# Expert tiles of 256, 320 and 128 tokens by rank, in place of 256 and 128 with one spare tile

## The chip, the cores and the metric

One core of one Trainium2 chip runs the whole program as one launch. The metric is the time of an execution on the device in microseconds. Three runs of the kernel before gave 782.85, 783.31 and 784.54 us.

## What is computed

Three layers follow each other: an attention within clusters (2 batches, 8 heads, 768 tokens, head size 64), a mixture of experts in which each token goes to one expert, and a bilinear layer. The middle one is what the change is about:

```python
logits = x @ w_gate                    # x: 1536 x 512, 8 experts
expert_idx = np.argmax(logits, axis=1)
...
    xe = x[mask]                       # the tokens of expert e
    h = np.maximum(xe @ w1[e], 0.0)    # 512 -> 1024
    ye = h @ w2[e]                     # 1024 -> 512
    out[mask] = gate_w[mask, None] * ye
```

How many tokens an expert has is known only when the attention has run. On the reference's own inputs, drawn with its default seed, experts 0 to 7 have 198, 119, 169, 188, 162, 192, 206 and 302 tokens.

## The kernel before

**Precision.** Matrix operands are kept as two parts, a rounded high part and the remainder ("hi" and "lo" for weights, "xh" and "xl" for tokens, "hh" and "hl" for the hidden layer), and each product is three matmuls. For a chunk of weights, which is 512 KB in a tile "raw", ACT casts "hi" (line 139) and DVE subtracts to get "lo" (line 145). An expert has eight chunks, four of w1 and four of w2.

**Routing.** Near the end of the attention the tokens are written to a buffer "xs" in DRAM, one region of 1536 rows for each expert, by indirect DMAs on POOL's queue (`scatter`). The first 256 rows of each region are set to zero earlier by DMAs from SP (line 888). `tables` then works out on DVE, from the counts, which expert stands at which place, where its output begins, and what is left over. Its first step is emitted at once, the others are spread over the expert stage, one for some of the calls of `tick`.

**The expert stage.** It goes through `SEQ` (line 72): nine places, 0, 1, 2, 7, 3, 8, 4, 5, 6. Places 0 to 6 are windows of 256 tokens (`window`, line 1088), with the tokens as the moving side: 96 matmuls of 256 columns for h, 96 for y. Place 7 is a tile of 128 tokens (`tile_of`, line 1140) with the weights as the moving side: 48 matmuls of 256 columns, eight transposes of h (line 1163), 24 matmuls of 512 columns (line 1176). It takes the expert with the fewest tokens. Place 8 is a tile of the same kind for the expert with most tokens beyond its window; it loads that expert's eight chunks once more, and its registers come from the table "wi". What is still left after that goes to a loop of 128-row tiles (line 1321), whose number of turns is read at run time. Expert 0 is always at place 0, since its weights are loaded before the counts are known.

**The order of work.** Each engine runs its instructions in the order in which they are written. `tick` is called 16 times in a window or a tile; each call lets `advance` split up to two more chunks, which puts a "hi" into ACT's queue and a "lo" into DVE's and lets SP issue the next load of "raw" (four buffers). The calls `nxt` in the second half of a window (`window(..., (1, 3))`) put in the transposes of the next place's tokens (`win_xt`, line 1075): four matmuls on PE into "xt", the copy "xh" on ACT, the subtraction "xl" on DVE. `store` (line 1134) copies y to "yt" in SBUF, two halves on ACT and DVE. A tile's output is transposed first ("yt_t", line 1203), in the next place.

**PSUM.** In the expert stage the tag "h" has four banks, "xt" two, and "y" takes two.

Of the kernel before, what the change touches and what calls it, by code (L numbers as in the profile page):

```python
# [23 lines left out]
W = 256  # L24
WS = 128
CH = 1024
# [3 lines left out]
def cluster_attention__then__moe__then__bilinear_kernel(  # L30
# [41 lines left out]
    SEQ = [0, 1, 2, E - 1, 3, E, 4, 5, 6]  # L72
    MOE2 = 8 * (E + 1)
# [85 lines left out]
    fmp = cp.tile([128, 128], F32, name="fmp")  # L159
# [8 lines left out]
    ahead = cp.tile([128, E, E], BF16, name="ahead")  # L168
    auxt = [cp.tile([128, NT, 2], U32, name=f"auxt{b}") for b in range(B)]

    def routing_constants():
        def iota(t, pattern, base=0, mult=0):
            nc.gpsimd.iota(t, pattern=pattern, base=base, channel_multiplier=mult,
                           allow_small_or_imprecise_dtypes=True)

        nc.gpsimd.memset(ones, 1.0)
# [11 lines left out]
        place_in = cp.tile([128, E], F32, name="place_in")  # L188
        n_s = SEQ.index(E - 1)
        nc.gpsimd.tensor_scalar(out=place_in, in0=ecol, scalar1=float(n_s), scalar2=1.0, op0=ALU.is_ge, op1=ALU.mult)  # L190
        nc.gpsimd.tensor_tensor(out=place_in, in0=place_in, in1=ecol, op=ALU.add)
        nc.gpsimd.memset(place_in[:, E - 1:E], float(n_s))
        nc.gpsimd.tensor_tensor(out=ahead, in0=place_in.unsqueeze(1).to_broadcast([128, E, E]),
                                in1=place_in.unsqueeze(2).to_broadcast([128, E, E]), op=ALU.subtract)
# [447 lines left out]
    def tables(later):  # L642
# [8 lines left out]
        m = cp.tile([128, 8], F32, name="wm")  # L651
        e1 = cp.tile([128, E], F32, name="we1")
        od = cp.tile([128, E], F32, name="od")
        nc.vector.tensor_reduce(out=m[:, 0:1], in_=cnt[:, 1:E], axis=AX.X, op=ALU.min)
        nc.vector.scalar_tensor_tensor(out=e1[:, 1:E], in0=cnt[:, 1:E], scalar=m[:, 0:1], in1=efirst[:, 0, 1:E],
                                       op0=ALU.is_le, op1=ALU.mult)
        nc.vector.tensor_reduce(out=m[:, 1:2], in_=e1[:, 1:E], axis=AX.X, op=ALU.max)
        nc.vector.tensor_scalar(out=m[:, 2:3], in0=m[:, 1:2], scalar1=-1.0, scalar2=float(E), op0=ALU.mult, op1=ALU.add)
        nc.vector.scalar_tensor_tensor(out=od, in0=ecol, scalar=m[:, 2:3], in1=ecol, op0=ALU.is_ge, op1=ALU.add)
        nc.vector.tensor_copy(od[:, E - 1:E], m[:, 2:3])  # L660
        ri = cp.tile([128, 3, E], I32, name="ri")
# [6 lines left out]
        hot = tp.tile([128, E, E], F32, name="hot")  # L668
        t8 = tp.tile([128, E, E], F32, name="t8")
        o8 = tp.tile([128, 2, E], F32, name="o8")  # L670
        off = cp.tile([128, E], F32, name="offs")
        nc.vector.tensor_tensor(out=hot, in0=od.unsqueeze(2).to_broadcast([128, E, E]),
                                in1=ecol.unsqueeze(1).to_broadcast([128, E, E]), op=ALU.is_equal)
# [6 lines left out]
        nc.vector.tensor_copy(ri[:, 2, :], o8[:, 1, :])  # L680
        yield
# [4 lines left out]


        cap = tp.tile([128, E], F32, name="cap")
        key = tp.tile([128, E], F32, name="key")
        nc.vector.tensor_scalar(out=cap, in0=hot[:, E - 1, :], scalar1=float(WS - W), scalar2=float(W),  # L690
                                op0=ALU.mult, op1=ALU.add)
        nc.vector.tensor_tensor(out=key, in0=cnt, in1=cap, op=ALU.subtract)
        nc.vector.tensor_scalar(out=key, in0=key, scalar1=0.0, scalar2=2048.0, op0=ALU.max, op1=ALU.mult)
        nc.vector.tensor_tensor(out=key, in0=key, in1=cnt, op=ALU.add)
        yield
        nc.vector.tensor_reduce(out=m[:, 0:1], in_=key, axis=AX.X, op=ALU.max)
        nc.vector.scalar_tensor_tensor(out=e1, in0=key, scalar=m[:, 0:1], in1=efirst[:, 0, :],
                                       op0=ALU.is_ge, op1=ALU.mult)
        nc.vector.tensor_reduce(out=m[:, 1:2], in_=e1, axis=AX.X, op=ALU.max)
        nc.vector.tensor_scalar(out=e1, in0=e1, scalar1=m[:, 1:2], scalar2=None, op0=ALU.is_equal)  # L700
        yield
        rs = cp.tile([128, E], F32, name="wrs")
        nc.vector.scalar_tensor_tensor(out=rs, in0=cnt, scalar=float(-WS), in1=cap, op0=ALU.add, op1=ALU.min)
        w3 = cp.tile([128, 3, E], F32, name="w3")
        nc.vector.tensor_tensor(out=w3[:, 1, :], in0=rs, in1=erow, op=ALU.add)
        nc.vector.tensor_tensor(out=w3[:, 2, :], in0=rs, in1=off, op=ALU.add)
        nc.vector.tensor_copy(w3[:, 0, :], ecol)
        nc.vector.tensor_tensor(out=w3, in0=w3, in1=e1.unsqueeze(1).to_broadcast([128, 3, E]), op=ALU.mult)
        wv = cp.tile([128, 3], F32, name="wv")
        nc.vector.tensor_reduce(out=wv, in_=w3, axis=AX.X, op=ALU.add)  # L710
        wi = cp.tile([128, 3], I32, name="wi")
        nc.vector.tensor_copy(wi, wv)
        regs["wi"] = wi
# [17 lines left out]
        nc.vector.tensor_scalar(out=n[:, 1:2], in0=n[:, 0:1], scalar1=1.0, scalar2=None, op0=ALU.is_gt)  # L731
        nc.vector.tensor_tensor(out=n[:, 0:1], in0=n[:, 0:1], in1=n[:, 1:2], op=ALU.mult)
# [337 lines left out]
    def win_load(w, src, n):  # L1070
        xw[w] = mp.tile([128, 2, DM], F32, tag="xw", name=f"xw{w}", bufs=2)
        for a in range(n // 128):
            nc.sync.dma_start(out=xw[w][:, a, :], in_=src[128 * a:128 * a + 128])

    def win_xt(w, n, a):

        if a == 0:
            xh[w] = mp.tile([128, DB, W], F32R, tag="xh", name=f"xh{w}", bufs=2)
            xl[w] = mp.tile([128, DB, W], F32R, tag="xl", name=f"xl{w}", bufs=2)
        x = mps.tile([128, 512], F32, tag="xt", name=f"xt{w}_{a}", bufs=2)  # L1080
        for d in range(DB):
            nc.tensor.transpose(x[:, 128 * d:128 * d + 128], xw[w][:, a, 128 * d:128 * d + 128], ident)
        xv = x.rearrange("p (d t) -> p d t", d=DB)
        oh, ol = xh[w][:, :, 128 * a:128 * a + 128], xl[w][:, :, 128 * a:128 * a + 128]
        nc.scalar.copy(out=oh, in_=xv)
        nc.vector.tensor_tensor(out=ol, in0=xv, in1=oh.bitcast(F32), op=ALU.subtract)

    def window(w, n, c0, tick, nxt, at):
        hh, hl = [], []
        y = mps.tile([128, DB, W], F32, tag="y", name=f"y{w}")  # L1090
# [15 lines left out]
        for fb in range(FB):  # L1106
# [364 lines left out]
```

## Time and profile before

| | |
|---|---|
| Runs | 782.85, 783.31, 784.54 us (median 783.31) |
| The profiled execution | 783.25 us, its span 781.1 us |
| Attention, routing | 0 to 279.4 us |
| Expert stage, first to last matmul | 279.36 to 475.29 us |
| Bilinear layer | 479.4 us to the end |
| PE busy in the span | 761.6 us (98%) |
| DVE, ACT, POOL busy | 523.2, 355.6, 156.9 us |

The profiled execution's time is 0.06 us below the median of the runs; the 2.15 us between its time and its span lie outside the instructions. Start times in the rows further down are from the span's start. Matmuls overlap in the pipeline, so the cost of one is read from the distance between starts, not from its duration.

### The profile page before, as it was taken

To read this page: it belongs to the slowest core of one execution; us is meant where nothing else is said; L and a number is where in the kernel's file an instruction comes from. 1 tells how busy PE (TensorE), PEld (TensorE's weight loads), DVE (VectorE), ACT (ScalarE), POOL (GpSimd) and SP (SyncE) were. 2 spreads that over 40 slices of the span, in tenths; PEclk is the share of its full clock that TensorE was granted. 3 is DMA by queue.
4 is the path that set the end of the run, shared out by engine and by line. 5 is a ranking of instruction groups with operands and counts; after the bars stand their busy time and mean duration, and the time that the engine had idled before them with its cause. 6 is when DMAs were issued, how large, how long until landed. Compare 5 with 4: busy or idle time off the path is not lost. (4 is left out here: it accounts for less than half of the span.)

```text
span 781.1 us, 12589 instructions
## 1 busy us (share of the span) xinstructions
PE 761.6 (98%) x4731; PEld 629.9 (81%) x4731; DVE 523.2 (67%) x947; ACT 355.6 (46%) x677; POOL 156.9 (20%) x164
## 2 busy tenths in 40 slices
PE   9999999999999999999999998999999999999996
PEld 8676676665766789998999997888888888888885
DVE  5867868778687778877686686766456765625323
ACT  6767666675666447547575432323132121210100
POOL 7623221415110410000007000211212112102011
PEclk9999999999999999999999999999999999999999
DMA  6685955737410168858789854322222220001011
GB/s 144 143 192 180 277 134 117 170 92 198 108 49 1 43 215 272 267 173 270 255 275 158 229 166 111 111 79 81 81 55 82 56 80 0 1 1 55 0 55 54
DMA packets 76302, 98.17 MB, mean 126 GB/s; under 512 B 28368, under 2 KB 49360, under 8 KB 76240
## 3 DMA queue, kind: packets, MB, share of 16 engines
q1 hardware_dynamic: 73792, 91.01, 42.2%
q0 software_dynamic: 2304, 6.31, 2.2%
q8 instruction: 38, 0.62, 0.4%
q14 instruction: 24, 0.20, 0.1%
q10 hardware_dynamic: 144, 0.03, 0.0%
HBM read 70.32 MB, written 10.50 MB: 103 GB/s over the span
## 5 line engine op out<-in xcount | busy, mean ns | idle before, releaser
L1408 PE MATMUL ab<-yh,hi 128*128 128x512 f32 x288 | 113.0, 392 | 0.0
L1408 PE MATMUL ab<-yh,lo 128*128 128x512 f32 x288 | 112.6, 391 | 0.0
L1415 DVE TENSOR_TENSOR ga<-ga,ab 128x512 f32<-128x512 f32 x36 | 24.7, 686 | 127.8 <-PE ab L1408 102.1
L464 DVE TENSOR_REDUCE nm<-s 128x1 f32<-128x768 f32 x96 | 91.5, 953 | 18.1 <-PE s L462 14.0
L145 DVE TENSOR_TENSOR lo<-raw,hi 128x1024 fp32r<-128x1024 f32 x70 | 84.8, 1223 | 22.4 <-ACT hi L139 21.7
L471 ACT ACTIVATE pr<-s,nm 128x768 f32<-128x768 f32 x96 | 87.0, 906 | 18.4 <-DVE nm L464 17.9
L462 PE MATMUL s<-ks,qs 128*128 128x512 f32 (+1 forms) x384 | 91.6, 361 | 0.3 <-ACT pr L471 0.3
L1414 ACT COPY ga<-ab 128x512 f32<-128x512 f32 x36 | 21.1, 586 | 151.9 <-PE ab L1408 151.9
L485 PE MATMUL t<-ident,pr 128*128 128x128 f32 x576 | 82.8, 277 | 3.8 <-DVE pt L491 2.2
L485 PEld LDWEIGHTS t<-ident,pr 128*128 128x128 f32 x576 | 64.6, 141 | 25.1 <-issue 10.8
L139 ACT CAST hi<-raw 128x1024 fp32r<-128x1024 f32 x70 | 72.2, 1048 | 17.4 <-DMA raw<-in_moe_w 17.3
L145 POOL TENSOR_TENSOR lo<-tmp,hi 128x512 fp32r<-128x512 f32 x28 | 38.2, 1365 | 204.6 <-ACT hi L139 204.6
L1408 PE MATMUL ab<-yl,hi 128*128 128x512 f32 x288 | 77.0, 389 | 0.0
L501 PE MATMUL o<-pt,vn 128*64 128x384 f32 (+1 forms) x432 | 74.5, 468 | 0.0
L491 DVE COPY pt<-t 128x384 f32<-128x384 f32 x94 | 51.8, 551 | 27.2 <-PE t L485 27.0
L489 ACT COPY pt<-t 128x384 f32<-128x384 f32 x98 | 46.7, 478 | 46.5 <-PE t L485 46.0
L462 PEld LDWEIGHTS s<-ks,qs 128*128 128x128 f32 x384 | 58.5, 190 | 9.6 <-issue 4.4
L1127 PE MATMUL y<-hh,hi 128*128 128x256 f32 x224 | 63.8, 285 | 0.0
L1408 PEld LDWEIGHTS ab<-yh,hi 128*128 128x128 f32 x288 | 54.5, 189 | 11.4
L1408 PEld LDWEIGHTS ab<-yh,lo 128*128 128x128 f32 x288 | 54.5, 189 | 11.3
L1408 PEld LDWEIGHTS ab<-yl,hi 128*128 128x128 f32 x288 | 54.1, 188 | 11.2
L1127 PE MATMUL y<-hh,lo 128*128 128x256 f32 x224 | 62.9, 281 | 0.0
(328 smaller groups left out, 1543.4 us busy)
## 6 DMA issues: line engine op xcount, KB each, us to landing
raw<-in_moe_w SPq DMA_DIRECT2D x72, 512.0 KB, 4.8
raw<-in_moe_w_a SPq DMA_DIRECT2D x12, 512.0 KB, 3.7
raw<-in_moe_w_b SPq DMA_DIRECT2D x12, 512.0 KB, 3.7
raw<-in_moe_w_out SPq DMA_DIRECT2D x12, 512.0 KB, 3.4
qs<-hiq SPq DMA_DIRECT2D x14, 384.0 KB, 4.8
ks<-hik SPq DMA_DIRECT2D x28, 192.0 KB, 4.8
xs<-zero SPq DMA_DIRECT2D x8, 512.0 KB, 5.5
xw<-xs SPq DMA_DIRECT2D x14, 256.0 KB, 5.0
```

The costliest lines, as they stand in the source:

```text
L139: nc.scalar.copy(out=hi, in_=raw)
L145: eng.tensor_tensor(out=lo, in0=raw, in1=hi.bitcast(F32), op=ALU.subtract)
L462: nc.tensor.matmul(sc[:, c0:c1], lhsT=w, rhs=ks[s, h][:, i, c0:c1], start=(i == 0), stop=(i == 1))
L464: nc.vector.tensor_reduce(out=nm, in_=sc[:, 0:S], axis=AX.X, op=ALU.max, negate=True)
L471: nc.scalar.activation(out=pr, in_=sc[:, 0:S], func=AF.Exp, bias=nm, scale=1.0, accum_out=sums[p][:, t, h:h + 1])
L485: nc.tensor.transpose(x[:, 128 * n:128 * n + 128], pr[:, 128 * kb:128 * kb + 128], ident)
L489: nc.scalar.copy(out=dst, in_=src)
L491: nc.vector.tensor_copy(dst, src)
L501: nc.tensor.matmul(o[64 * h:64 * h + 64, 0:n], lhsT=vn[:, h, kb, :], rhs=pt_t[p, g, h][:, kb, 128 * j0:128 * j0 + n], start=(kb == 0), sto ...
L1127: nc.tensor.matmul(y[:, d, 0:n], lhsT=a_[:, fb % 2, 128 * d:128 * d + 128], rhs=b_[:, 0:n], start=(fb == 0 and d % 2 == 0 and i == 0), sto ...
L1408: nc.tensor.matmul(p_, lhsT=a_[:, d, f0:f0 + 128], rhs=b_[d], start=(i == 0), stop=(i == len(seq) - 1))
L1415: nc.vector.tensor_tensor(out=ga, in0=ga, in1=ab[1], op=ALU.mult)
```

## The change

`SEQ` has eight places instead of nine, in the order of their numbers. The experts are ranked by their number of tokens on DVE (expert 0 first, always; the others by count). Place 1 takes the fullest of the others and is a window of 320 columns; place 3 takes the emptiest and is the tile of 128; the rest are windows of 256. The spare tile, its table "wi" and its loads are gone; what does not fit goes to the loop, now from the first tile on. A window of 320 loads a third piece of 64 rows ("xw1b"), transposes it in a third call of `nxt`, and accumulates y in four banks, two of "y" and two of "h", which `store_wide` copies with eight instructions. SP also sets 64 more rows of each expert's region to zero.

```diff
+WL = 320
...
-    SEQ = [0, 1, 2, E - 1, 3, E, 4, 5, 6]
-    MOE2 = 8 * (E + 1)
+    LARGE, LITTLE = 1, 3
+    RANK = [0, 1, 2, E - 1] + list(range(3, E - 1))
+    SIZE = [WL if n == LARGE else WS if n == LITTLE else W for n in range(E)]
+    SEQ = list(range(E))
+    MOE2 = 8 * E
...
+        nc.vector.scalar_tensor_tensor(out=key, in0=cnt, scalar=8.0, in1=ties, op0=ALU.mult, op1=ALU.add)
+        nc.vector.tensor_tensor(out=more, in0=key.unsqueeze(1).to_broadcast([128, E, E]),
+                                in1=key.unsqueeze(2).to_broadcast([128, E, E]), op=ALU.is_gt)
+        nc.vector.tensor_reduce(out=rank, in_=more, axis=AX.X, op=ALU.add)
+        nc.vector.tensor_tensor(out=hot, in0=by_rank.unsqueeze(2).to_broadcast([128, E, E]),
+                                in1=rank.unsqueeze(1).to_broadcast([128, E, E]), op=ALU.is_equal)
+        nc.vector.tensor_tensor(out=t8, in0=hot, in1=ecol.unsqueeze(1).to_broadcast([128, E, E]), op=ALU.mult)
+        nc.vector.tensor_reduce(out=od, in_=t8, axis=AX.X, op=ALU.add)
...
-        nc.vector.tensor_scalar(out=n[:, 1:2], in0=n[:, 0:1], scalar1=1.0, scalar2=None, op0=ALU.is_gt)
-        nc.vector.tensor_tensor(out=n[:, 0:1], in0=n[:, 0:1], in1=n[:, 1:2], op=ALU.mult)
...
+        at(NU + 2 + 2 * e, lambda e=e: nc.sync.dma_start(
+            out=xs[e * NTOK + W:e * NTOK + WL, :].rearrange("r (h d) -> (r h) d", h=2), in_=zero[:, 0:DM // 2]))
...
     def win_load(w, src, n):
...
+        if n > W:
+            xw[w].append(mp.tile([128, DM], F32, tag="yn", name=f"xw{w}b"))
+        for a in range(-(-n // 128)):
+            m = min(128, n - 128 * a)
+            nc.sync.dma_start(out=xw[w][a][0:m], in_=src[128 * a:128 * a + m])
...
     def window(w, n, c0, tick, nxt, at):
...
+        if n > W:
+
+            ys = [y.rearrange("p d t -> p (d t)")[:, 512 * i:512 * i + n] for i in range(2)]
+            ys += [mps.tile([128, 512], F32, tag="h", name=f"y{w}_{i}", bufs=4)[:, 0:n] for i in range(2)]
...
+    def store_wide(ys, n, at, at2):
+        for d in range(DB):
+            copy = nc.scalar.copy if d < 2 else nc.vector.tensor_copy
+            copy(out=yt[:, d, bass.ds(at, W)], in_=ys[d][:, 0:W])
+            copy(out=yt[:, d, bass.ds(at2, n - W)], in_=ys[d][:, W:n])
...
-        if t < 18 and t % 4 == 2 or 18 <= t < 48 and t % 2 == 0 or t >= 97:
+        if t < 18 and t % 4 == 2 or 18 <= t < 48 and t % 2 == 0 or t >= 16 * (LITTLE + 1) + 2:
...
-            y = window(r, W, 8 * pos, tick, nxt, (1, 3))
-            store(y, W, ov[r])
+            y = window(r, size(r), 8 * pos, tick, nxt, (1, 3, 5))
+            if size(r) > W:
+                store_wide(y, size(r), ov[r], ov[r, 1])
+            else:
+                store(y, W, ov[r])
```

How this moves instructions stands below for two places. The first is ACT's queue in the second half of place 0, where the tokens of place 1 are prepared ("xh1" from the transposes "xt1") between the casts of chunks 12 to 15 and the store of place 0. Before:

```order
L1085 CAST xh1_3708<-xt1_0_3710 128x4x128
L139 CAST hi_12_3719<-raw_12_3611 128x1024
L1256 TENSOR_LOAD ri_3422
L1085 CAST xh1_3708<-xt1_1_3753 128x4x128
L139 CAST hi_13_3760<-raw_13_3653 128x1024
L139 CAST hi_14_3766<-raw_14_3676 128x1024
L139 CAST hi_15_3798<-raw_15_3682 128x1024
L1135 ISA
L1135 COPY yt_3449<-y0_3487 128x2x256
L1116 ACTIVATE hh1_0_3853<-h1_0_3840 128x256
```

And of the change:

```order
L1082 CAST xh1_3722<-xt1_0_3724 128x4x128
L143 CAST hi_12_3734<-raw_12_3625 128x1024
L1264 TENSOR_LOAD ri_3436
L1082 CAST xh1_3722<-xt1_1_3768 128x4x128
L143 CAST hi_13_3775<-raw_13_3667 128x1024
L143 CAST hi_14_3781<-raw_14_3690 128x1024
L1082 CAST xh1_3722<-xt1_2_3811 128x4x64
L143 CAST hi_15_3820<-raw_15_3696 128x1024
L1143 ISA
L1143 COPY yt_3463<-y0_3501 128x2x256
L1114 ACTIVATE hh1_0_3875<-h1_0_3862 128x320
```

A third piece of "xh1" now stands behind the casts of chunks 13 and 14, and the first matmul of place 1 reads all 320 columns of "xh1".

The second place is SP's queue at the start of place 0, where the tokens of place 1 are loaded ("xw1") ahead of chunks 8 and on. Before:

```order
L102 DMA raw_7_3472<-in_moe_w2 128x2x512
L1256 TENSOR_LOAD ri_3422 x3
L1073 ISA
L1073 DMA xw1_3527<-xs_70 128x512
L1073 ISA
L1073 DMA xw1_3527<-xs_70 128x512
L102 ISA
L102 DMA raw_8_3561<-in_moe_w1 128x4x256
```

And of the change:

```order
L106 DMA raw_7_3486<-in_moe_w2 128x2x512
L1264 TENSOR_LOAD ri_3436 x3
L1069 ISA
L1069 DMA xw1_3541<-xs_70 128x512
L1069 ISA
L1069 DMA xw1_3541<-xs_70 128x512
L1069 ISA
L1069 DMA xw1b_3542<-xs_70 64x512
L106 ISA
L106 DMA raw_8_3575<-in_moe_w1 128x4x256
```

The load of the third piece, 64 rows or 128 KB, has moved in ahead of chunk 8.

## Rows read from the trace of the kernel before

**Rows 1.** The page: busy time and share of the span, of PE.
```profile
PE 761.6 (98%) x4731; PEld 629.9 (81%) x4731; DVE 523.2 (67%) x947; ACT 355.6 (46%) x677; POOL 156.9 (20%) x164
```

**Rows 2.** Windows view by place, columns as the first line: place 1, both tiles, all nine.
```profile
core 0: us, PE busy (x) PEld busy (x) DVE busy (x) ACT busy (x) POOL busy (x), PEclk, DMA share, GB/s
...
303.91:328.05 24.14, 24.04 (x203) 23.84 (x201) 22.12 (x55) 15.00 (x22) 0.00 (x0) 1.00 0.85 277
...
351.39:365.50 14.11, 13.25 (x90) 11.85 (x89) 10.61 (x14) 11.33 (x17) 0.00 (x0) 1.00 0.86 290
...
389.27:402.52 13.25, 13.24 (x90) 11.85 (x89) 11.41 (x14) 11.30 (x17) 0.00 (x0) 1.00 0.76 253
...
sum 195.93, PE 193.19 PEld 189.58 DVE 150.36 ACT 109.20 POOL 14.63; mean PE 21.47 PEld 21.06 DVE 16.71 ACT 12.13 POOL 1.63
```

**Rows 3.** Waits of PE from 276 to 482 us: total us, times, longest.
```profile
PE warm L790 <- SPq L1321: 2.3, 1, 2.3
...
PE xt L1082 <- issue: 0.9, 1, 0.9
PE h L1103 <- ACT xh L1240: 0.7, 1, 0.7
```

**Rows 4.** Timeline of PE, expert stage: start, duration, instruction, count.
```profile
303.91 0.29 PE L1103 MATMUL h<-xh,hi 128*128 128x256 f32 x1
...
401.12 0.40 PE L1176 MATMUL y<-hi,sh 128*128 128x512 f32 x1
...
402.52 0.28 PE L1103 MATMUL h<-xh,hi 128*128 128x256 f32 x1
...
414.04 0.28 PE L1127 MATMUL y<-hh,hi 128*128 128x256 f32 x1
...
417.35 0.60 PE L1082 MATMUL xt<-ident,xw 128*128 128x128 f32 x4
417.71 0.36 PE L1127 MATMUL y<-hh,hi 128*128 128x256 f32 x1
```

**Rows 5.** The chain that ended last, in order of time, bilinear layer: start, us, count.
```profile
494.33 5.44 PE ab L1408 x24
```

**Rows 6.** Timeline of ACT, end of place 0; in brackets idle before, and its releaser.
```profile
303.79 1.05 ACT L139 CAST hi<-raw 128x1024 fp32r<-128x1024 f32 x1 [0.94 <-DMA raw<-in_moe_w]
305.10 1.06 ACT L139 CAST hi<-raw 128x1024 fp32r<-128x1024 f32 x1 [0.26 <-DMA raw<-in_moe_w]
306.06 0.57 ACT L1135 COPY yt<-y 128x512 f32 x1
306.53 0.38 ACT L1116 ACTIVATE hh<-h 128x256 fp32r<-128x256 f32 x1
```

**Rows 7.** Timeline of DVE, ends of places 0 and 1.
```profile
304.87 1.22 DVE L145 TENSOR_TENSOR lo<-raw,hi 128x1024 fp32r<-128x1024 f32 x1 [0.76 <-ACT hi L139]
...
328.25 0.69 DVE L1136 COPY yt<-y 128x512 f32 x1 [0.71 <-PE y L1127]
```

**Rows 8.** Timeline of SP's DMA issues, attention and start of place 0.
```profile
61.54 2.25 SPq L888 DMA_DIRECT2D xs<-zero  x3
74.19 2.68 SPq L428 DMA_DIRECT2D qs<-hiq  x2
...
285.00 0.94 SPq L1073 DMA_DIRECT2D xw<-xs  x2
```

**Rows 9.** Timeline of PE, attention.
```profile
188.75 0.55 PE L485 MATMUL t<-ident,pr 128*128 128x128 f32 x3 [0.35 <-ACT pt L489]
190.62 0.55 PE L485 MATMUL t<-ident,pr 128*128 128x128 f32 x3 [1.33 <-DVE pt L491]
```

**Rows 10.** Windows view of the stretch behind those two waits (columns as rows 2).
```profile
191.25:195.17 3.92, 3.92 (x15) 1.58 (x14) 2.71 (x5) 1.93 (x4) 2.92 (x3) 0.56 0.78 282
```

**Rows 11.** DMA issues of the page: queue, count, KB each, median us to landing.
```profile
raw<-in_moe_w SPq DMA_DIRECT2D x72, 512.0 KB, 4.8
...
xw<-xs SPq DMA_DIRECT2D x14, 256.0 KB, 5.0
```

More of the change, by code (lines that the diff above doesn't have):

```diff
@@ L168, in cluster_attention__then__moe__then__bilinear_kernel @@
     ahead = cp.tile([128, E, E], BF16, name="ahead")
+    by_rank = cp.tile([128, E], F32, name="by_rank")
+    ties = cp.tile([128, E], F32, name="ties")
     auxt = [cp.tile([128, NT, 2], U32, name=f"auxt{b}") for b in range(B)]
@@ L174, in iota @@
                            allow_small_or_imprecise_dtypes=True)
+        fmp = ap.tile([128, 128], F32, name="fmp")
         nc.gpsimd.memset(ones, 1.0)
@@ L186, in routing_constants @@
         iota(jcol, [[0, E], [1, NJ]])
[L188 to L194, printed above, removed]
-        nc.gpsimd.tensor_scalar(out=ahead, in0=ahead, scalar1=0.0, scalar2=1.0, op0=ALU.is_lt, op1=ALU.mult)
+        nc.gpsimd.tensor_tensor(out=ahead, in0=ecol.unsqueeze(1).to_broadcast([128, E, E]),
+                                in1=ecol.unsqueeze(2).to_broadcast([128, E, E]), op=ALU.subtract)
+        nc.gpsimd.tensor_scalar(out=ahead, in0=ahead, scalar1=0.0, scalar2=1.0, op0=ALU.is_lt, op1=ALU.mult)
+        iota(by_rank, [[1, E]])
+        nc.gpsimd.memset(by_rank[:, LITTLE:LITTLE + 1], float(E - 1))
+        iota(by_rank[:, LITTLE + 1:E], [[1, E - LITTLE - 1]], LITTLE)
+        iota(ties, [[-1, E]])
+        nc.gpsimd.memset(ties[:, 0:1], float(16 * NTOK))
         for b in range(B):
@@ L649, in tables @@
         nc.vector.tensor_copy(cnt, c[:, 0:E])
[L651 to L661, printed above, removed]
+        key = ap.tile([128, E], F32, name="key")
+        more = ap.tile([128, E, E], F32, name="more")
+        rank = cp.tile([128, E], F32, name="rank")
+        hot = cp.tile([128, E, E], F32, name="hot")
+        t8 = ap.tile([128, E, E], F32, name="t8")
+        od = ap.tile([128, E], F32, name="od")
+        nc.vector.scalar_tensor_tensor(out=key, in0=cnt, scalar=8.0, in1=ties, op0=ALU.mult, op1=ALU.add)
[6 more added lines that the diff above has]
+        nc.vector.tensor_reduce(out=od, in_=t8, axis=AX.X, op=ALU.add)
+        ri = cp.tile([128, 4, E], I32, name="ri")
         nc.vector.tensor_copy(ri[:, 0, :], od)
@@ L667, in tables @@
         tp = later()
[L668 to L669 removed]
+        t8 = tp.tile([128, E, E], F32, name="t8b")
         o8 = tp.tile([128, 2, E], F32, name="o8")
         off = cp.tile([128, E], F32, name="offs")
[L672 to L673 removed]
         nc.vector.tensor_tensor(out=t8, in0=hot, in1=cnt.unsqueeze(1).to_broadcast([128, E, E]), op=ALU.mult)
@@ L680, in tables @@
         nc.vector.tensor_copy(ri[:, 2, :], o8[:, 1, :])
+        nc.vector.tensor_scalar(out=ri[:, 3, :], in0=o8[:, 1, :], scalar1=float(W), scalar2=float(NTOK + W - (WL - W)),
+                                op0=ALU.add, op1=ALU.min)
         yield
@@ L688, in tables @@
         cap = tp.tile([128, E], F32, name="cap")
[L689 to L713, printed above, removed]
+        e1 = cp.tile([128, E], F32, name="we1")
+        nc.vector.tensor_scalar(out=cap, in0=rank, scalar1=float(RANK[LARGE]), scalar2=float(WL - W),
+                                op0=ALU.is_equal, op1=ALU.mult)
+        nc.vector.tensor_scalar(out=e1, in0=rank, scalar1=float(RANK[LITTLE]), scalar2=float(WS - W),
+                                op0=ALU.is_equal, op1=ALU.mult)
+        nc.vector.tensor_tensor(out=cap, in0=cap, in1=e1, op=ALU.add)
+        nc.vector.tensor_scalar(out=cap, in0=cap, scalar1=float(W), scalar2=None, op0=ALU.add)
         yield
@@ L1090, in window @@
         y = mps.tile([128, DB, W], F32, tag="y", name=f"y{w}")
+        ys = [y[:, d, 0:min(n, W)] for d in range(DB)]
         seqs = [[(i, d) for d in range(DB) for i in range(2)] + [(2, d) for d in range(DB)]]
@@ L1142, in tile_of @@
         hp_ = [mps.tile([128, 512], F32, tag="h", name=f"h{w}_{i}", bufs=4) for i in range(2)]
-        hs = mp.tile([128, F], F32, tag="ys", name="hs", bufs=2)
-        hh = [mp.tile([128, W], F32R, tag=f"hh{i}", name=f"sh{i}") for i in range(FB // 2)]
-        hl = [mp.tile([128, W], F32R, tag=f"hl{i}", name=f"sl{i}") for i in range(FB // 2)]
+        hs = mp.tile([128, F], F32, tag="ys", name="hs")
+        hh = [mp.tile([128, WL], F32R, tag=f"hh{i}", name=f"sh{i}") for i in range(FB // 2)]
+        hl = [mp.tile([128, WL], F32R, tag=f"hl{i}", name=f"sl{i}") for i in range(FB // 2)]
         def h_part(c):
@@ L1194, in tile_of @@
             y_part(fb)
-        yn = mp.tile([128, F], F32, tag="ys", name="yn", bufs=2)[:, 0:DM]
+        yn = mp.tile([128, DM], F32, tag="yn", name="yn")
         nc.scalar.copy(out=yn, in_=y)
```

50 lines of the change are left out of this document (25 added, 25 removed).

## The prediction

> **What bounds the kernel now.** The page comes first: PE is busy for 98% of the span, with DVE at 67% and ACT at 46% [rows 1]. So a change is worth what it takes from PE's queue or puts in front of it. The windows view, cut at the first matmul of each place, says the same of the expert stage: of its 195.93 us PE is busy for 193.19 [rows 2]. PE's waits make up the rest. Two of them matter here: 0.9 us in front of the transposes "xt" inside the tile of place 3, which is why that tile takes 14.11 us and the spare one 13.25 [rows 2, 3], and 2.3 us at the loop's entry, which the change leaves alone [rows 3].
>
> The distances between starts give PE's price of a column. Six matmuls of 512 columns go from 401.12 to 402.52, 0.233 us each, and the next 96 of 256 columns from 402.52 to 414.04, 0.120 us each [rows 4]. In the bilinear layer 24 of 512 columns take 5.44 us, 0.227 each [rows 5]. So 256 columns more cost 0.107 to 0.113 us, and 64 columns a quarter of that, 26.7 to 28.3 ns.
>
> **The spare tile goes.** Its stretch lasts 13.25 us [rows 2]. It also holds the two transposes of the next place's tokens, which stay; but its own one and that of its output, which stand in the places before and after, go with it, and four transposes cost the same 0.36 us (417.35 to 417.71) either way [rows 4]. The sum: **-13.25 us**. Its eight chunks, 4.2 MB, their casts and subtractions go too. I cost that at nothing, since PE did not wait for them elsewhere in the stage.
>
> **The wide window.** It has 192 matmuls with 64 columns more: 192 x 26.7 to 28.3 ns is 5.1 to 5.4 us. I take **+5.3**, nearer to the price seen in this stage. The third piece of its tokens needs four transposes of 64 rows, between half and the whole of 0.36 us [rows 4]: **+0.3**.
>
> The first of these terms is where a rule speaks against the rows. In a stream of weight loads and matmuls the distances are 0.120 and about 0.23 us here [rows 4, 5]. The Trainium skill ("TensorE: Matmul & The Clock Gate", Back-to-back issue gap) gives 81 ns at 128 columns and 131 ns at 512 for such a stream. By that, 64 columns cost 8 ns, the wide window an estimated 1.6 us, and the sum below would be 3.7 us better. The trace disagrees by its 0.227 and 0.233, and I go by the trace.
>
> **A new wait at the start of place 1.** Each engine keeps its order, so the place of the third copy "xh1" counts. It stands behind ACT's casts of chunks 13 and 14 (order of ACT above). In the trace the second of these waits 0.94 us for its weights and runs from 303.79 to 304.84, at the very end of place 0; the next matmul of PE starts at 303.91 [rows 4, 6]. The cast of chunk 15 and the store of y followed there, and the store began at 306.06 although y had been ready for two microseconds: this is what standing behind a late chunk costs [rows 6]. None of it held PE, because no next matmul needed it. Now one does. The third copy has 256 elements to a partition, as the activation of 0.38 us [rows 6], and can end at 305.2 at the earliest; place 1 would be ready at 303.91 + 0.3 = 304.2. PE waits 1.0 us. The third subtraction "xl1" stands behind "lo" of chunk 14, which ended at 306.09 [rows 7]; it ends by 306.5, and PE needs it eight matmuls after 305.2, at 306.4: 0.1 more. Third, SP now issues the extra load ahead of chunk 8 (order of SP above); an issue takes 0.47 us [rows 8], and if chunk 14 becomes late by all of that, so does PE. From below: if chunk 14 landed 0.94 us earlier, the wait would be gone. So 0 to 1.6 us, and I take **+1.2**.
>
> **What I cost at nothing.**
> - The banks. Two of the wide window's y products use banks of "h", and the third h of place 2 waits until DVE has copied them. It starts 24 x 0.120 = 2.9 us after place 2 does. DVE's copies have 640 columns in four instructions; before, 512 columns took 0.69 us, and DVE had been idle for 0.71 us when it began [rows 7]. Even twice 0.69 leaves 1.5 us of cover. If DVE came to that point later than this cover, PE would wait in place 2.
> - DVE in place 1. It was busy for 22.12 of 24.14 us [rows 2]. The place now lasts 5.3 us longer with hardly more to do, so the weights, loaded at a share of 0.85 [rows 2], get ahead rather than fall behind.
> - The ranking. DVE has eight small instructions for it where eight were before, some with 64 elements instead of 8. PE's first wait in the stage is for ACT's "xh", 0.7 us [rows 3], which needs none of them.
> - Eight more zeroing DMAs on SP. They cost no more than the larger ones, 2.25 us for three [rows 8], some 6 us in all. After the last of those three SP has nothing to issue until 74.19. If one did push back a load of "qs", the cover is the distance by which the preparation of a pair of heads runs ahead. On POOL, net one constant more; it idles for 80% of the span [rows 1].
> - The tile at place 3 keeps its 0.9 us [rows 3].
>
> **The sum.** -13.25 + 5.3 + 0.3 + 1.2 = -6.45 us. Against the profiled execution's 783.25 that is **776.8 us**. Its time is within 0.1 us of the median of the runs, so nothing is added. The unknown terms bound this case: 5.1, 0.2 and 0 give 775.3; 5.4, 0.36 and 1.6 give 777.4. A measurement of this kernel tells 0.2%, or 1.6 us, from no change.
>
> **Rivals.**
> 1. *The third copy is in time.* Chunk 14 lands earlier, since the order of loads or their neighbours shift. Then PE waits for nothing: 775.6. For it: the lateness is only 0.94 us. Against it: one more load goes ahead of chunk 14, none fewer. 12%.
> 2. *The wait takes the clock down.* In the attention PE waited 0.35 and 1.33 us in a row, and in the stretch behind that the granted clock was 0.56, half rate for most of it [rows 9, 10]. Its 3.92 us held 0.56 of the work, so 1.7 us were lost. A wait of 1.2 us at 304 could do the same: 778.5. Against it: the tile's 0.9 us and the first 0.7 us of the stage [rows 3] left the clock at 1.00 in the places after [rows 2]. 13%.
> 3. *Columns are free.* PE's weight loads are busy for 23.84 of 24.14 us [rows 2]. If they set the pace, 64 columns cost nothing: 783.25 - 13.25 + 0.3 + 1.2 = 771.5. Against it: with the same weight loads, 512 columns take 0.107 us or more longer than 256 [rows 4, 5]. 3%. The rule of the Trainium skill named above would put it at 773.1.
> 4. *The loop turns.* The change takes away the spare tile and lets whatever does not fit go to the loop from the first tile on. On the reference's own inputs the ranking gives 302 tokens to 320 columns, 119 to 128, and 206 at most to 256, so the loop has no turn; before, 302 - 256 = 46 tokens went to the spare tile. If the fullest expert had 321 tokens, or the ranking put another in place 1, there would be a turn. It loads 4.2 MB through two buffers: eight loads at 4.8 us to landing, in pairs or one by one, 19 to 38 us, and about two short loads of 5.0 before them [rows 11]: 29 to 48 us. That ends **slower**, at 806 to 825. 3%. It also stands for the case that the change does not do what it says.
> 5. *More late banks or chunks.* The cover of the banks is overrun, or the chunks after the extra load are late as well: one to three microseconds more, 778 to 780. 6%.
> 6. *The half rate in the attention is gone or comes twice* [rows 10]: 1.7 us less or more, 775.1 or 778.5. 5%.
>
> **How the numbers follow.** My forecast has the remaining 58%, and its value, 776.8, is the prediction. The range goes from 774.9 to 779.5: it takes in rivals 1 and 2, both sides of 6, and most of 5. Left out are rivals 3 and 4 and a tail on either side, some 14% together. Only the loop, and a heap of mishaps that each would have to cost three times its bound, lead to no gain: faster 0.94, within 0.2% 0.02, slower 0.04.
>
> **What would show it.** In the profile of the changed kernel, the expert stage should take about 189.5 us from first to last matmul, with the bilinear layer as long as before. The distance of the 320-column matmuls should be 0.147 us. PE's waits should have a new entry, "h" on ACT's "xh", of about 1.2 us, where place 1 begins; no such entry speaks for rival 1. A granted clock under 1.00 just behind it speaks for rival 2, matmuls closer than 0.14 us for rival 3, and any instruction of the loop's body for rival 4. Waits of "h" on the copies into "yt" in place 2 would say that the cover of the banks was judged wrongly. An expert stage over 193 us without any of these would make the account itself wrong.

## The result, and the profile after

The changed kernel took **774.25 us** (median of four runs, 773.54 to 776.04), the kernel before beside it 783.08 (781.85 to 784.54): a ratio of **0.9891** (0.9867 to 0.9916). A second series, run e8 below, had 775.18 and 782.53: 0.9911 (0.9888 to 0.9933). The forecast was 776.8 with a range from 774.9 to 779.5. The direction was right; the gain was 8.8 us in the first series and 7.4 in the second where 6.45 were forecast, and the first median lies 0.65 us below the range, the second inside it.

The profiled execution took 773.54 us, its span is 771.8. The page's first part, as [rows 1], and the windows view of the expert stage, cut at the first matmul of each place, as [rows 2]:

```profile
PE 752.1 (97%) x4647; PEld 621.9 (81%) x4647; DVE 511.6 (66%) x924; ACT 345.6 (45%) x664; POOL 154.9 (20%) x166
```

```profile
core 0: us, PE busy (x) PEld busy (x) DVE busy (x) ACT busy (x) POOL busy (x), PEclk, DMA share, GB/s
280.96:306.73 25.77, 24.87 (x205) 24.27 (x205) 20.69 (x33) 16.12 (x25) 0.00 (x0) 1.00 0.76 251
306.73:336.04 29.31, 29.31 (x201) 29.14 (x202) 22.08 (x49) 15.08 (x24) 0.00 (x0) 1.00 0.72 227
336.04:359.37 23.33, 23.33 (x199) 23.33 (x198) 16.99 (x39) 11.90 (x20) 0.00 (x0) 1.00 0.62 193
359.37:372.70 13.33, 13.29 (x91) 11.84 (x89) 11.43 (x14) 11.24 (x17) 0.00 (x0) 1.00 0.79 267
372.70:397.19 24.49, 24.37 (x205) 24.27 (x204) 16.35 (x27) 13.10 (x21) 11.31 (x11) 1.00 0.94 201
397.19:420.98 23.79, 23.79 (x203) 23.79 (x201) 15.20 (x20) 12.49 (x19) 1.23 (x1) 1.00 0.89 226
420.98:444.76 23.78, 23.78 (x202) 23.78 (x201) 16.32 (x24) 11.93 (x19) 0.00 (x0) 1.00 0.74 233
444.76:467.68 22.92, 22.92 (x195) 22.92 (x193) 19.76 (x36) 7.16 (x16) 0.00 (x0) 1.00 0.52 163
sum 186.72, PE 185.66 PEld 183.34 DVE 138.81 ACT 99.01 POOL 12.55; mean PE 23.21 PEld 22.92 DVE 17.35 ACT 12.38 POOL 1.57
```

The stage is 195.93 - 186.72 = 9.21 us shorter. Place 1 costs 5.17 more than its 24.14 [rows 2], and the spare tile's 13.25 are gone, as forecast. Place 0, which ends with the wait for the third copy, grew by 1.22 (it was 24.55) where 1.5 were forecast, but its parts are others. Two things were not forecast at all. The tile of place 3 takes 13.33 in place of 14.11. And the windows behind it no longer wait. Before, the last three stood at:

```profile
402.52:426.73 24.21, 24.21 (x206) 24.20 (x204) 17.08 (x30) 13.04 (x21) 12.59 (x11) 1.00 0.92 221
426.73:451.13 24.40, 23.94 (x202) 23.73 (x200) 14.46 (x21) 12.16 (x19) 1.69 (x2) 1.00 0.93 212
451.13:475.29 24.16, 23.27 (x193) 23.07 (x194) 21.41 (x39) 7.05 (x16) 0.00 (x0) 1.00 0.58 175
sum 72.77, PE 71.42 PEld 71.01 DVE 52.95 ACT 32.25 POOL 14.28; mean PE 23.81 PEld 23.67 DVE 17.65 ACT 10.75 POOL 4.76
```

PE was busy for 71.42 of those 72.77 us; in the last three of the changed kernel for all of 70.49. PE's waits say it too, of the kernel before (those beside [rows 3]) and of the changed one, from 276 us to the loop's entry (total, times, longest):

```profile
PE h L1103 <- DVE hl L1117: 1.3, 2, 0.9
...
PE h L1103 <- ACT xh L1085: 0.5, 1, 0.5
```

```profile
PE warm L780 <- SPq L1333: 2.1, 1, 2.1
PE h L1101 <- ACT xh L1248: 0.7, 1, 0.7
PE h L1101 <- DVE hl L1115: 0.7, 1, 0.7
...
PE h L1101 <- ACT xh L1082: 0.2, 1, 0.2
```

The last line is the new wait for the third copy: 0.2 us, not 1.2. Outside the stage the differences cancel. Part of them are stretches in which TensorE ran at 1.2 GHz in place of 2.4, "half clock" from here on; each costs some 1.7 us. Leaving out the last three microseconds, the kernel before has two, behind 191 us [rows 10] and at the start of the bilinear layer, the changed one a single one, at the end of the attention. Windows view, of the kernel before (start of the bilinear layer) and of the changed one (end of the attention, start of the bilinear layer):

```profile
479.38:491.62 12.24, 12.24 (x51) 10.06 (x51) 8.71 (x16) 2.21 (x4) 2.22 (x2) 0.91 0.29 51
```

```profile
270.80:273.93 3.13, 3.13 (x27) 2.68 (x27) 1.09 (x8) 0.63 (x2) 0.00 (x0) 0.55 0.53 168
...
471.11:482.29 11.18, 11.18 (x52) 9.26 (x51) 9.19 (x16) 2.50 (x5) 2.22 (x2) 1.00 0.31 55
```

The stretch from the stage's last matmul to the end of the first 48 products "ab" is 1.72 us shorter. But the stage starts 1.60 us later, since ahead of the new stretch PE waited 1.8 us longer in front of "xo". PE in both:

```profile
269.43 0.48 PE L529 MATMUL xo<-iw,ot 128*128 128x144 f32 x2 [0.37 <-ACT pt L489]
```

```profile
269.73 0.48 PE L537 MATMUL xo<-iw,ot 128*128 128x144 f32 x2 [2.17 <-DVE sel L604]
```

This wait is not the change's doing: it is 2.14 to 2.26 us in thirteen of the fourteen traces of this case, e7's of the kernel before among them, and the first trace of the kernel before is the exception. The stretches at half clock come and go between executions of one kernel, so part of any difference is chance. Of the executions whose mean granted clock was 0.999, which leaves no room for such a stretch, the three of the kernel before in e8's series took 780.41, 780.55 and 781.47, the changed kernel's one 773.27: 7.1 us and more remain.

### The profile page after: what moved, and what is told of

It is laid out like the page before. It is cut to its first block, busy times and chain, and to the rows that moved or that the text cites. A ratio compares the mean times of both kernels' runs of the same rounds, so it can differ in the third digit from the quotient of the medians.

```text
span 771.8 us, 12348 instructions
## 1 busy us (share of the span) xinstructions
PE 752.1 (97%) x4647; PEld 621.9 (81%) x4647; DVE 511.6 (66%) x924; ACT 345.6 (45%) x664; POOL 154.9 (20%) x166
## 5 line engine op out<-in xcount | busy, mean ns | idle before, releaser
L149 DVE TENSOR_TENSOR lo<-raw,hi 128x1024 fp32r<-128x1024 f32 x62 | 75.4, 1224 | 20.9 <-ACT hi L143 19.0
L143 ACT CAST hi<-raw 128x1024 fp32r<-128x1024 f32 x62 | 64.3, 1048 | 14.0 <-DMA raw<-in_moe_w 13.7
L1129 PE MATMUL y<-hh,hi 128*128 128x256 f32 (+1 forms) x224 | 64.9, 290 | 0.0
L1129 PE MATMUL y<-hl,hi 128*128 128x256 f32 (+1 forms) x224 | 63.7, 284 | 0.1
L1129 PE MATMUL y<-hh,lo 128*128 128x256 f32 (+1 forms) x224 | 63.7, 285 | 0.0
```

The lines of the kernel that those rows point to most:

```text
L143: nc.scalar.copy(out=hi, in_=raw)
L149: eng.tensor_tensor(out=lo, in0=raw, in1=hi.bitcast(F32), op=ALU.subtract)
L1129: nc.tensor.matmul(ys[d], lhsT=a_[:, fb % 2, 128 * d:128 * d + 128], rhs=b_[:, 0:n], start=(fb == 0 and (d % 2 == 0 or n > W) and i == 0), ...
```

## The experiments

Two questions: why do the last windows no longer wait, and what does place 0 pay? Two suspects stood for the first. The twelve indirect writes of "aux" by POOL move with the change: 410.5 to 427.8 before, 378.6 to 397.3 after. And the spare tile, which uses two chunks a step, is gone.

**e1: the changed kernel, writes of aux later.**

```
-    ... or t >= 16 * (LITTLE + 1) + 2:
+    ... or t >= 16 * (LITTLE + 2) + 2:
```

> The changed kernel with one number changed: the steps of the tables that end in the twelve small writes of 'aux' start 16 calls of tick later, in place 5 instead of place 4, so that they stand as far from the end of the expert stage as in the kernel before. Theory A (the writes of 'aux' stand in the way of the weights, and their distance from the end decides whether the last two places wait): places 6 and 7, 23.78 and 22.92 us in the changed kernel, get back 1.2 to 1.5 us together, with waits of PE's h on DVE's hl or ACT's xh; the stage goes from 186.7 to about 188. Theory B (the spare tile, which uses up weights at twice the pace shortly before, caused those waits, and the writes do not matter): the stage stays within 0.4 us of 186.7, and no such wait appears.

774.17 us. The writes went out from 402.5 to 421.2, 46 us ahead of the stage's end, as before the change (47.5), and no late wait came back: the last three places took 23.85, 23.78 and 22.92. So the position of the writes alone does not make the waits. Place 0 had a wait of its own, 1.1 us of the third transposes for a bank that DVE had not emptied (xt <- DVE xl), which the forecast had at nothing; e11, the same kernel again, did not have it.

**e2: the kernel before, writes of aux earlier.**

```
-    ... or t >= 97:
+    ... or t >= 66:
```

> The kernel before with the same number changed the other way: the writes of 'aux' start at call 66 instead of 97, right behind the first tile, as in the changed kernel. Theory A: the windows of places 7 and 8 (24.40 and 24.16 us before) come down to about 23.8 and 22.9, the stage from 195.9 to 194.2 to 194.7, if the spare tile does not now wait for weights itself. Theory B: those two windows keep their 0.5 and 0.9 us of waits, and the stage stays at 195.5 to 196.3.

790.18 us, one execution, beside a single one of the kernel before with 780.99. Part of that distance is chance: e2 has three stretches at half clock, and the other, at a mean granted clock of 0.999, none. The stage tells more: 201.12 us in place of 195.93. The last three windows lost their waits (24.20, 23.78, 22.91), but the spare tile, now just behind the writes, took 21.50 us in place of 13.25. Windows view of that tile, and PE's waits from 386 to 412:

```profile
390.01:411.51 21.50, 15.36 (x90) 12.86 (x89) 11.49 (x14) 11.71 (x17) 3.08 (x4) 0.92 0.87 217
```

```profile
PE xt L1082 <- issue: 2.7, 1, 2.7
PE y L1176 <- ACT sh L1165: 1.4, 1, 1.4
PE ht L1163 <- ACT hs L1158: 1.2, 1, 1.2
PE y L1176 <- DVE sl L1167: 0.8, 1, 0.8
```

ACT stood behind casts that waited 1.6 to 2.7 us each for weights. Behind the last of them DVE's "sl" came late as well, which empties the bank that the first line waits for (it ends at 408.16, "xt" starts at 408.26). Of the tile and the writes, whichever comes second pays.

**e5: the kernel before, the remaining steps of the tables behind the last window.**

```
-    ... 18 <= t < 48 and t % 2 == 0 or t >= 97:
+    ... 18 <= t < 48 and t % 2 == 0:
...
+    for _ in tab_steps:
+        pass
     keep_warm(2, "xt", [128, 512], 2, mps)
```

> The kernel before, with the remaining steps of the tables (the gates, the rows of the loop and the twelve writes of aux) taken out of the windows and put behind the last one. So far the late waits (the last three windows of the kernel before took 72.77 us against 70.89 without them) went away when the twelve writes were moved ahead of the spare tile, and did not come back when they were moved behind in the changed kernel. Theory A, the writes alone cause them: the last three windows take 70.9 us, and the spare tile 13.25. Theory B, the spare tile's chunks alone (two a step) cause them: the last three windows stay at 72.8. Theory C, they need both, the chunks that the tile has used up and the writes that keep the loads from catching up: the last three windows take 70.9, as by A; A and C are told apart by the run with the writes moved late in the changed kernel, which by A should have had the waits and had none. The end after the last window is later by all three, by 10 to 25 us, since the writes and the table of the loop are waited for there; that is not looked at.

The last three windows took 70.89 us, with the spare tile at 13.26 (801.69 in all, since the end waits for the writes). Theory A and C agree here, and e1 speaks against A: the writes as far from the end as before do no harm where no spare tile stands ahead of them. (No run takes the spare tile alone out of the kernel before: e1 also has the ranking and the wide window. And e5 moves the other steps of the tables along with the writes.) How the writes do it stands in the DMA issues from 405 to 440 us (KB each, median us from issue to landing), of the kernel before and of e5:

```profile
raw<-in_moe_w SPq DMA_DIRECT2D x11, 512.0 KB, 8.2
```

```profile
raw<-in_moe_w SPq DMA_DIRECT2D x11, 512.0 KB, 3.8
```

The loads land in 8.2 us in place of 3.8 (in e3, 3.7 from 300 to 372 us and 10.0 beside the writes, from 372 to 400). The chunks are then late: ACT's casts of the last ones waited up to 2.40 us, for the loads themselves, so the small steps on DVE are not what holds them up. DVE's work for the bilinear weights ("tmp") crowds behind them, and the products of the last window wait for "hl". Timeline of DVE around that window's first "hl", of the kernel before (window from 451.13) and of the changed one (from 444.76):

```profile
446.93 1.23 DVE L145 TENSOR_TENSOR lo<-raw,hi 128x1024 fp32r<-128x1024 f32 x1 [1.14 <-ACT hi L139]
...
457.56 1.09 DVE L1117 SCALAR_TENSOR_TENSOR hl<-h,hh 128x256 fp32r<-128x256 f32 x3 [0.25 <-ACT hh L1116]
```

```profile
437.59 2.36 DVE L149 TENSOR_TENSOR lo<-raw,hi 128x1024 fp32r<-128x1024 f32 x2 [0.26 <-ACT hi L143]
...
449.42 1.09 DVE L1115 SCALAR_TENSOR_TENSOR hl<-h,hh 128x256 fp32r<-128x256 f32 x3 [0.31 <-ACT hh L1114]
```

The "lo" of the last chunk ends 3.0 us ahead of the window before (446.93 + 1.23 against 451.13) and 4.8 after, and the first "hl" begins 6.4 us behind the window's start against 4.7.

**e7: the kernel before again.** No edit.

> The kernel before once more, unchanged, for a second trace of it. If the late waits (the last three windows at 72.8 us in place of 70.9) and the 0.9 us in front of the transposes inside the tile of place 3 belong to the kernel, both are there again, with the tile at 14.1 us. If they are chance of one execution, the last three windows take 70.9 us and the tile 13.3. The runs with the writes of aux moved had the tile at 13.3 to 13.4 both times, so the 0.9 us is expected to be chance, and the late waits not.

783.30 us, stage 193.98 in place of 195.93. The tile of place 3 took 13.56 and the last three windows 71.42; PE waited for "hl" again in the last one, but 0.26 us in place of 0.9:

```profile
353.18:366.74 13.56, 13.25 (x90) 11.85 (x89) 10.66 (x14) 11.46 (x17) 0.00 (x0) 1.00 0.90 303
```

```profile
451.75:475.18 23.43, 23.17 (x195) 22.97 (x194) 20.69 (x38) 7.05 (x16) 0.00 (x0) 1.00 0.58 178
```

The 0.9 us in the tile varies from execution to execution (0.3 here, none in e2 and e5). It too is a late chunk: the bank of the transposes is emptied by DVE's "sl", which stood behind a "lo" whose weights came late. DVE and PE in the first trace:

```profile
361.41 0.75 DVE L1167 TENSOR_TENSOR sl<-ht,sh 128x256 fp32r<-128x256 f32 x2
```

```profile
362.26 0.63 PE L1082 MATMUL xt<-ident,xw 128*128 128x128 f32 x4 [0.86 <-issue]
```

The late waits are there in both traces of the kernel, but their size varies: 1.88 us over e5's 70.89 in the first, 0.53 in this one, where the last chunk's "lo" ended 3.7 us ahead of the last window in place of 3.0.

**e3: the wide window at place 5. e4: the third transposes one block of y later.**

```
-    LARGE, LITTLE = 1, 3
-    RANK = [0, 1, 2, E - 1] + list(range(3, E - 1))
+    LARGE, LITTLE = 5, 3
+    RANK = [0, 4, 2, E - 1, 3, 1, 5, 6]
...
-            y = window(r, size(r), 8 * pos, tick, nxt, (1, 3, 5))
+            y = window(r, size(r), 8 * pos, tick, nxt, (1, 3, 6))
```

The first four lines are e3's (with the ranks of places 1 and 5 set in by_rank and a buffer of its own for the third piece), the last two e4's.

> The changed kernel with the window of 320 at place 5, behind the tile, in place of 1 (its third piece of tokens in a buffer of its own). Theory A (the wide window in front of the tile gives the weights 5.2 us more, and that is why the tile's wait of 0.9 us is gone): the tile at place 3 takes about 14.1 us again instead of 13.3, with PE waiting 0.8 to 0.9 us in it, and place 1 about 24.1. Theory B (the wait in the tile hung on something else, such as the longer tables or the place of single loads): the tile stays at 13.3. For the third copy: at place 5 no cast ahead of it waits for weights, so PE should not wait for it there.

> The changed kernel with the third piece of tokens of the wide window transposed one step later in place 0, so that its copy on ACT stands behind the cast of chunk 15 as well. Theory A (PE starts the wide window when that copy is done, and what stands ahead of it on ACT sets the time): PE's wait at the start of place 1 grows from 0.23 us to 1.1 to 1.5, place 0 and 1 together from 55.1 to 56.1 to 56.5 us. Theory B (place 0 ends late by itself, and the copy has slack to spare): the wait stays under 0.5 us.

e3: 773.55 us, stage 186.10; no wait for the third copy at all, place 0 at 24.80, and the wide window at 29.03. The tile is at 13.31 without a wide window ahead of it, so it is not the wide window that mends the tile. e4: 776.19 us; the wait for the third copy became 1.5 us, with the clock at 1.00 behind it:

```profile
PE h L1101 <- ACT xh L1082: 1.5, 1, 1.5
```

So the mechanism of the forecast is there; one block of y, twelve matmuls, decides its size.

**e6: 256 columns for the fullest too, its 46 further tokens to the loop.**

```
-WL = 320
+WL = 256
...
-        at(NU + 2 + 2 * e, lambda e=e: nc.sync.dma_start(
-            out=xs[e * NTOK + W:e * NTOK + WL, :]...
```

> The changed kernel with 256 columns for the fullest expert as for the others, without its third 64 rows and without the zeroing of those rows: its 46 tokens beyond 256 go to the loop after the windows, one turn. Both theories expect place 1 at 24.1 us in place of 29.3, no third transposes and no third copy in place 0 (24.8 us in place of 25.8: of the 1.2 us over the kernel before, 0.26 of a wait for hl stays), and the last three windows as in the changed kernel (70.5 us), since there is no spare tile. The stage then takes 186.7 - 5.2 - 1.0 = 180.5 us. The turn of the loop was priced at 29 to 48 us in the prediction's rival 4: the time is 773.5 - 6.2 + 29 to 48 = 796 to 815 us. If the turn costs under 6.2 us the wide window is not worth its columns; if it is 29 or more, the wide window is what makes leaving the spare tile out possible.

804.89 us. Place 0 took 24.73 and place 1 23.87. The way from the last window to the first "ab" shows what one turn of the loop costs:

```profile
460.14:500.29 40.15, 24.54 (x145) 20.63 (x143) 4.33 (x13) 3.94 (x11) 0.00 (x0) 0.79 0.39 118
```

The changed kernel has 3.43 us there (467.68 to 471.11), so a turn costs 36.7 us in this one execution, stretches at half clock included, and lies inside the 29 to 48 of rival 4. The 64 columns for 5.2 us are what makes it possible to leave the spare tile out.

**e8 to e10, and e11 and e12: timed beside each other.** e8 is the changed kernel again. e9 has keep_warm(14, ...) in place of keep_warm(2, ...) at the end of the stage, e10 the same with e3's edit, e11 is e1 again, and e12 is e3 with the writes from place 6 on (LITTLE + 3).

> The changed kernel once more, unchanged, beside the two variants of this call. Both theories: 774 us, ratio to the kernel before 0.989. Its places 4 to 7 take 95.0 us and its tile 13.3 again. Place 0 depends on when the stage starts: at 281.0 us it took 25.8, at 279.3 us 26.9, since the third transposes wait for a bank until DVE has its chunk; if the attention ends without the stretch at half clock, place 0 is the 1.1 us longer.

> The changed kernel with 14 in place of 2 matmuls that only keep PE at work ahead of the loop, where PE is idle for 2.1 us and where three of six traces show a stretch of 3.4 us at half the clock right behind it (1.7 us lost). Theory A, the idle time is what lets the clock fall there: the stretch is gone in this run, the 12 more matmuls lie within the 2.1 us, and the time is up to 1.7 us below the changed kernel's when that has the stretch, 0 when not. Theory B, PE's idle time begins only after its own matmuls (it waits for a register that is loaded behind them): the time rises by the 12 matmuls, 0.8 to 1.8 us, and the stretch at half clock comes as often.

> The wide window at place 5 in place of 1, so that the third transposes fall into place 4, where the chunks are ahead, and the 14 matmuls at the end. With the wide window there the stage took 186.1 us from 279.0, against 186.7 from 281.0 and 187.8 from 279.3 with it at place 1. Theory A, what the third transposes cost in place 0 comes from the chunks that are late there: 0.6 to 1.7 us below the changed kernel of this call, plus or minus what the matmuls at the end do. Theory B, it was chance: the same time as the changed kernel within 0.5 us.

> The changed kernel with the writes of aux from the start of place 5 on in place of the start of place 4, timed. In three traces of the changed kernel place 4, in which the twelve writes lie, took 24.49, 25.20 and 27.13 us; with the writes in place 5 it took 24.21, and place 5 itself 23.85, no more than without them. In the longest one PE stood for 2.2 us in front of matmuls that waited for nothing that the profile shows, and the DMA moved 91 GB/s. Theory A, the writes right behind the tile of place 3 hold PE up there: the times fall by 0.3 to 2.9 us, by their mean 1.4 (ratio to the kernel before 0.989 against the 0.991 of the last series), and the spread of the executions, 773.3 to 778.8, becomes narrower; place 4 is 24.2 in the trace. Theory B, these waits have nothing to do with the writes: ratio 0.991, the same spread, and waits of that kind in any place. The late waits of the kernel before (0.5 to 1.9 us in its last three windows) are not expected back by either.

> The wide window at place 5 and the writes of aux from the start of place 6 on. If third transposes cost in place 0 because the chunks are late there, and the writes hold PE up in place 4, both are gone: place 0 takes 24.8 us, place 4 some 24.4 (third transposes included), places 6 and 7 46.7 in sum, the stage 185.5 to 186, which is 1.2 us below the changed kernel's shortest (186.72) and 4.0 below its longest (189.52): a ratio to the kernel before of 0.987 to 0.989, and the fastest version of all. If the writes now make the last windows wait, as they did in the kernel before, places 6 and 7 take 47.2 to 48.6 and the ratio is 0.990.

| run | median us (lowest to highest, runs) | ratio to the kernel before |
|---|---|---|
| e8, changed kernel | 775.18 (773.27 to 778.80, 6) | 0.9911 (0.9888 to 0.9933) |
| e9, warm end | 779.24 (777.84 to 782.57, 12) | 0.9964 (0.9948 to 0.9980) |
| e10, wide at 5, warm end | 779.26 (777.08 to 781.58, 7) | 0.9956 (0.9940 to 0.9971) |
| e11, writes at place 5 | 775.60 (771.17 to 778.03, 6) | 0.9917 (0.9893 to 0.9941) |
| e12, wide at 5, writes at place 6 | 777.01 (774.51 to 783.05, 12) | 0.9939 (0.9917 to 0.9961) |

e8's profiled execution, at 778.80, shows where the changed kernel can lose: its place 4, in which the writes now lie, took 27.13 us, and in the worst six microseconds of it PE issued 29 matmuls (45 in five in the first trace), waiting for nothing that the profile names, while the DMA moved 91 GB/s:

```profile
373.43:400.56 27.13, 24.93 (x205) 24.52 (x204) 15.33 (x26) 12.80 (x21) 14.06 (x12) 1.00 0.82 195
...
392.00:398.00 6.00, 3.80 (x29) 3.40 (x28) 1.23 (x1) 0.18 (x2) 3.83 (x4) 1.00 0.64 91
```

With the writes in place 5 (e1, e11) place 4 took 24.21 both times, but e11's times are e8's. The expected 1.4 us is less than the interval of either series can show; e11's spread is no narrower and runs along with the granted clock (spans of 769.4 at 0.998, 776.3 at 0.992). What holds PE up in e8 stays open. The longer place 0 of e1 does not: e8's expectation put it down to an early start of the stage, but e11's stage starts as early (279.46) and its place 0 took 25.37 us. It is again a late chunk: the cast that DVE's work stood behind waited 1.81 us for its load in e1 (at 299.59), and none of the chunk casts from 295 to 304 us waited more than 0.66 in e11.

e9's theory B came true in its mechanism: PE's idle time begins behind its own matmuls. Its price did not, 4.1 us where 0.8 to 1.8 were expected. Timeline of PE from the stage's end to the first "ab":

```profile
467.74 3.29 PE L780 MATMUL warm<-ident 128*128 128x128 f32 x28
473.17 0.60 PE L780 MATMUL warm<-ident 128*128 128x128 f32 x3 [2.14 <-DVE yl L1393]
474.78 1.01 PE L780 MATMUL warm<-ident 128*128 128x128 f32 x3 [1.01 <-issue]
475.45 0.77 PE L1420 MATMUL ab<-yh,hi 128*128 128x512 f32 x1
```

(The trace counts each of these matmuls twice.) The 2.14 us are as long as before, the way is 7.71 us in place of 3.43, and the stretch at half clock there was 6.8 us long, where e8 has one of 3.4 and the changed kernel's first trace none. e10 pays the same; beside e9 the wide window at place 5 gains nothing that these series show, where its theory A expected 0.6 to 1.7 us. In e12 the last window of a kernel without a spare tile waited again, now that the last write went out 27 us ahead of the end; "hl" was 1.80 us late, and the clock fell behind it:

```profile
445.14:471.59 26.45, 24.65 (x194) 24.45 (x193) 20.93 (x38) 7.17 (x16) 0.43 (x1) 0.94 0.72 190
```

Its ratio, 0.9939, is behind the 0.990 that was expected for that case. So the writes make the late waits, and two things decide if there is reserve: what the loads were spent on ahead of them (the tile's eight chunks) and how much of the stage is left behind them. No version was faster than the changed kernel by more than the intervals.

## Why the prediction came out as it did

- **The spare tile, -13.25.** Right: the stretch is gone.
- **"I cost that at nothing, since PE did not wait for them elsewhere in the stage."** This is the step that failed. The view of waits behind [rows 3] had two further lines, 1.3 us for "hl" and 0.5 for "xh", 0.9 and 0.46 of them in the last two windows. They are the bill of chunks that the tile had used up and the writes of aux kept from landing in time (e5 and e12 for the writes; e1 and e11 for the tile, within what was said at e5). With the tile they went: 1.88 us in this pair of traces, 0.53 by e7. So the term was worth 0.5 to 1.9 us, and how much of the distance to the range it makes up is not shown, since the second series lies inside the range.
- **"The tile at place 3 keeps its 0.9 us."** Failed too, by 0.78 us in this pair. e7 and the tiles of e2 and e5 show that it comes and goes in the kernel before as well, so it should have been in the range and not in the value. That it fell to the changed kernel's credit is luck of this pair.
- **The wide window, +5.3.** Measured 5.17 (e3: 29.03 against 23.78 for the place behind it, 5.25); the 320-column matmuls stand 0.147 us apart, those of 256 columns 0.120. The Trainium skill ("TensorE: Matmul & The Clock Gate", Back-to-back issue gap), by which it would have cost an estimated 1.6, does not hold for this stream.
- **The third transposes, +0.3.** From 302.81 to 303.41 PE takes 0.60 us where two products of y stand 0.12 apart: 0.48.
- **The new wait at place 1, +1.2.** The mechanism is there (e4: 1.5 us), its size was wrong: 0.23 us, and about 0.4 with PE's restart. Timeline of ACT, to be read against [rows 6]:

```profile
305.35 1.05 ACT L143 CAST hi<-raw 128x1024 fp32r<-128x1024 f32 x1 [0.35 <-DMA raw<-in_moe_w]
306.31 0.36 ACT L1082 CAST xh<-xt 128x256 fp32r<-128x256 f32 x1
306.65 1.05 ACT L143 CAST hi<-raw 128x1024 fp32r<-128x1024 f32 x1
```

  Chunk 14's cast starts 24.39 us after the stage does (24.43 before), as late as assumed, and the third copy ends 25.71 us after it, where 25.84 were forecast (305.2 - 279.36). So the end of the wait was right. What was wrong is when PE comes to it. The forecast had 0.3 us for the transposes as cover; it was 0.48 for them and 0.26 for "hl" (next point). These costs were paid inside the wait and made it shorter, and the extra load did not make chunk 14 later. The sum for place 0 came within 0.3 us because the mechanism was right; the split into its parts was not.
- **"The ranking" at nothing.** The first wait for "hl" in place 0 went from 0.41 to 0.67 us, and 0.6 to 0.7 in the changed kernel's other traces. DVE's subtractions for place 0 start 0.47 us into the stage in place of 0.21, behind the ranking, and its first "hl" 6.21 in place of 5.95. PE's first wait was indeed not touched; a later one was.
- **The banks** held in place 2, but e1's 1.1 us in place 0 is a bank that a late chunk kept full, which I had not looked at.
- **Rivals.** 1 came nearest. 2 did not happen at 304, but e12 shows its mechanism, 1.80 us of waiting and then half clock; e4's 1.5 us did not do it. 3 and 4 fell; e6 confirms 4's price. 6 was right about the size, 1.7 us, but had one such stretch in mind: the kernel before has two in both its traces, and in the changed kernel's first trace the one behind 191 us is gone and another came at 271.

In this pair the terms are -13.25 + 5.17 + 1.22 - 0.78 - 1.56 - 0.01 = -9.21, the sum of the places. -1.56 is places 4 to 7 against the windows that stood there: 1.88 of late waits, less 0.3 that place 4, in which the writes now lie, became longer. Against the forecast's -6.45 that is 2.76 better: 1.56 from these windows, 0.78 from the tile, 0.28 from place 0, 0.13 from the wide window. The pair of e7 and e8 has 193.98 and 189.52, only 4.5 apart, with e8's slow place 4. The forecast of 189.5 for the stage lies at the upper end of the changed kernel's traces: 186.72, 187.40 (e9, which differs only behind the stage) and 189.52 (e8).

## What to carry to other kernels

When work is taken out of a tuned pipeline, read every line of the wait view behind it, however short: a wait some windows later can be the removed work's bill, paid in loads that it used up ahead of time. Small scattered writes are priced by what they do to the loads beside them, and by how far ahead those loads are of the work that reads them. When a new wait ends at a fixed time, every cost ahead of it shortens it, so forecast the time at which it ends. And take a second trace of the kernel before, ahead of the forecast: 0.9 us in a tile and 1.8 us in front of "xo" differ between two traces of it.

## What the hardware showed beyond that

- Twelve indirect writes of 128 rows of 8 bytes each bring 512 KB loads beside them from 3.8 to 8.2 us to landing (e5 and the kernel before, 405 to 440 us).
- A stretch at half clock costs 1.7 us, and the same wait is followed by it in one execution and not in another. All fourteen traces have the waits of 0.34 and 1.33 us in the attention [rows 9]; in seven the granted clock fell to half behind them, in seven it stayed at 1.00. The 2.17 us in front of "xo" were followed by it in the changed kernel's first trace, the 2.14 to 2.26 us at the same place in twelve others were not. In the expert stage 1.80 us did in e12, 1.5 in e4 did not.
- Matmuls that only keep PE at work ahead of its wait shorten nothing: 12 more of them cost 4.1 us on the median (e9 against e8), and in both traces with them (e9, e10) the stretch at half clock was twice as long as e8's.
